# One order for all units, earlier split units, padding from a row: a scheduler change to a fused FFT and SwiGLU kernel

## The chip, the cores and the metric

The kernel runs on one core of one Trainium2 chip. The metric is the device time of one execution in microseconds (us), lower is better. The kernel before takes 624.05 us (median of three runs, 622.47 to 624.16). In what follows PE is TensorE, DVE is VectorE, ACT is ScalarE, POOL is GpSimd and SP is SyncE, which issues most loads and stores.

## The reference, cut to what matters

```python
# x: (8, 3008, 256) float32;  w_gate, w_val: (256, 1536);  w_out: (1536, 256)
X = np.fft.fft(x, axis=1)
X = np.fft.fft(X, axis=2)
x = X.real.astype(np.float32).reshape(8 * 3008, 256)

g = x @ w_gate
silu = g * (1.0 / (1.0 + np.exp(-g)))
val = x @ w_val
return (silu * val @ w_out).astype(np.float32)        # (24064, 256)
```

## The kernel before: the parts that matter here

The Fourier transform over the sequence is done as matmuls with cosine and sine tables, on data folded by symmetry. The transform over the 256 channels is multiplied into the gate and value weights once, at the start (`transform_w`, giving `Wp`, `Wq`, `Wm`). Each batch has a half of its rows (1504) computed directly, and the other half is its mirror image: with P the even and Q the odd part, one half is P·Wp + Q·Wq and its mirror P·Wp − Q·Wq.

The columns are cut into 24 tiles of up to 512, and each tile into 12 units of 128 hidden channels. A unit is computed in one of two ways.

- A **whole** unit takes six matmuls: gate and value, each with Wp, Wq and, for the mirror, Wm (= −2·Wq) accumulated on top. It needs two Silu on ACT and two products on DVE.
- A **split** unit takes five. The mirrored value is worked out on DVE from the value itself: `es` is a copy of the P part with the share of one row of Q added, and the mirrored value is 2·es − v. That needs this row of Q (`br`, then `bc`) broadcast to all partitions by two small loads, and more work on DVE, ACT and POOL. A unit split in its gate as well takes four.

Before the change, tiles 0 to 2 were all whole units, in a fixed order of emission. From tile 3 on, a small list scheduler inside the kernel (`Sched`) ordered them. It keeps one list of operations for each engine, with estimated durations, and picks the operation that can start first within a window.

The first batch's rows arrive in two arrays, `XA` and `XC0`. `XC0` has 60 rows in each half of 64 partitions. The four spare partitions must be zero, because a matmul with a 0/1 matrix ("placing") reads them all. Row 0 of the sequence is loaded into the first spare partition.

```python
    nc.vector.memset(zero, 0.0)
    nc.vector.memset(sel, 0.0)
    q.dma_start(out=XA3[:, 0:4, :], in_=up_block(0, 1, P))
    for a, eng in ((3, nc.scalar), (1, nc.scalar), (2, q), (0, q)):
        eng.dma_start(out=XA3[:, 4 + a, :], in_=down_set(0, a, JA, LA, NA))
    nc.scalar.activation(w0[:, 0, 0:1], zero, AF.Silu)
    xf = XC0.rearrange("p a q d -> p (a q d)")
    nc.scalar.copy(xf, zero.to_broadcast([P, xf.shape[1]]))       # all of XC0 zeroed on ScalarE
    for hi in range(2):
        q.dma_start(out=XC3[64 * hi:64 * hi + NCR, 0:2, :], in_=rows_at(...))
    q.dma_start(out=XC0[NCR:64 + NCR + 1:64, 0:2, 1], in_=rows_at(0, 0, ...))   # row 0
    for hi in range(2):
        for a in range(2):
            q.dma_start(out=XC3[64 * hi:64 * hi + NCR, 2 + a, :], in_=down_set(...))
    ...                                    # XC's padding: four loads from a zero row of XC0

    psA = place(XA, putA, 4, ((psG, "g"), (psV, "v")))
    ...
    half_folded(0, 0)
    psC = place(XC0, putC, 2, ((psO, "o"),))
    half_folded(0, 2)
    ...
    wts0 = [...]       # all eight products for the first third of Wp, Wq
    sums(SC, 1, XC0, psC)
    halves(SBc, SC, 1)
    for fn in wts0:
        fn()
```

The scheduler's rule for when an operation can start:

```python
            def ready(o):
                at = 0.0
                for d in o.deps:
                    x = ops[d]
                    if x.end is None:
                        return None
                    at = max(at, x.end + (0.03 if x.eng == o.eng and x.eng != "SP" else x.lat))
                ...                                             # buffers
                return at
```

The last tile's output matmuls accumulate 12 products for each block of 128 rows, two blocks to a PSUM bank, in the pool `psO` of two banks:

```python
        def product(self, st, pair, j, minus, c, n, f, t):
            if "ps" not in st:
                st["ps"] = psO.tile([P, 2, D], F32, name="o")
            nc.tensor.matmul(st["ps"][:n, j, :], hts[t][minus][:, f, c:c + n], Wo[:, f, :],
                             start=(f == 0), stop=(f == nF - 1))
```

## Time and profile before

| | before |
|---|---|
| median of three runs | 624.05 us |
| span of the profiled run | 621.6 us |
| PE busy | 604.1 us (97%) |
| DVE, ACT, POOL busy | 91%, 85%, 73% |
| first placing of XC0, first gate matmul | 13.33, 23.47 us |
| last matmul starts, span ends | 616.37, 621.57 us |

These are lines of the page of the kernel before: span, busy time of each engine, PE's busy share and granted clock in 40 equal slices (9 is 90% or more), and the chain of work that ended last, by engine and by line.

```profile
span 621.6 us, 12538 instructions
...
PE 604.1 (97%) x4020; PEld 394.0 (63%) x4080; DVE 568.3 (91%) x1042; ACT 526.8 (85%) x999; POOL 453.6 (73%) x421
...
PE   7889999999999999999999999999999999999996
...
PEclk9999999999999999999999999999999999999999
...
PE 88%; DMA 4%; DVE 3%; ACT 2%; issue 2%; POOL 0%; ACTq 0%; SPq 0%; DVEq 0%
PE o L1082 38%; PE g L876 25%; PE v L876 20%; DMA XA<-in_moe_w_val_dram 2%; PE g L1241 2%; PE o L1241 2%; DMA XA<-in_x_dram 1%; DMA XC<-in_x_dram 1%; DVE sv L1028 1%; DVE hp L1038 1%; DVE es L969 0%; PE o L567 0%; PE g L567 0%; ACT sv L1014
```

PE bounds the kernel. Only the first three slices and the last are under 90%, the clock is full throughout, and 88% of the chain is matmuls. So time can be won by fewer matmuls, and at the two ends.

Next are the first 50 us of the kernel before in the waits of PE: who waited for what, us in total, times, longest.

```profile
PE v L876 <- DVE hp L892: 2.3, 5, 0.9
PE g L408 <- DVE rr L331: 1.9, 1, 1.9
...
PE g L876 <- DVE Qt L603: 0.7, 1, 0.7
```

And the first 32 us of its chain (start us, us, what) show what sets the start:

```profile
1.42 7.91 DMA XA<-in_x_dram
...
9.34 0.84 SPq L252
...
10.22 6.21 DMA XC<-in_x_dram
...
16.55 0.71 DVE SC L417 x2
```

Loads do. One of XA's ends at 9.3, and the last of XC0's (L252) is issued then and lands at 16.4. The timeline of the same stretch (start us, us, engine, line, operation) shows the copy that the change takes out, the loads behind it, and the first placing of XC0 and the first gate matmul:

```profile
3.46 1.88 ACT L244 COPY XC<-zero 128x2048 f32<-128x2048 f32 x1
...
5.37 0.82 SPq L246 DMA_DIRECT2D XC<-in_x_dram  x2
...
7.00 4.05 SPq L252 DMA_DIRECT2D XC<-in_x_dram  x4
...
13.33 1.88 PE L408 MATMUL o<-XC,putC 128*128 128x512 f32 x4
...
23.47 0.37 PE L876 MATMUL g<-Pt,Wp 128*128 128x480 bf16 x1
```

Tiles 1 and 2 run from about 50 to 110 us. A row of the windows view gives start and end, length, busy time of PE, of PE's weight loads, of DVE, ACT and POOL with counts, then granted clock, DMA share and GB/s. Kernel before:

```profile
50.00:110.00 60.00, 59.68 (x408) 38.37 (x413) 42.12 (x73) 37.06 (x68) 38.71 (x48) 1.00 0.44 121
```

DVE is busy 42.1 of 60 us there, and PE loses almost nothing.

At the end, the only wait of PE in the kernel before is for an eviction:

```profile
PE o L1082 <- ACT ev L1088: 0.7, 1, 0.7
```

### The profile page before, as it was taken

How to read it: one execution, taken by the hardware profiler on the slowest of the kernel's cores; microseconds unless marked ns; L12 is line 12 of the kernel's file. 1: busy time of each engine (PE TensorE's matmuls, PEld its weight loads, DVE VectorE, ACT ScalarE, POOL GpSimd, SP SyncE). 2: the span in 40 equal slices, each digit the busy share in tenths (PEclk: the TensorE clock that was granted, in tenths of full speed). 3: DMA queues.
4: the chain of work that ended last, by engine and by line, in shares of the span. 5: the costliest groups of instructions: out<-in, count | busy, mean ns of one | idle time of the engine just before them, and what ended most of it. 6: DMA issues, size and time to landing. Idle time of an engine off the chain costs nothing.

```text
span 621.6 us, 12538 instructions
## 1 busy us (share of the span) xinstructions
PE 604.1 (97%) x4020; PEld 394.0 (63%) x4080; DVE 568.3 (91%) x1042; ACT 526.8 (85%) x999; POOL 453.6 (73%) x421
## 2 busy tenths in 40 slices
PE   7889999999999999999999999999999999999996
PEld 5346666666666666566666666666666666666684
DVE  7798567999999999999999999999999999999981
ACT  7686666899889889888898889998898988989992
POOL 8896955888877989886988779868786434545551
PEclk9999999999999999999999999999999999999999
DMA  9973346345326223546153113144211211111121
GB/s 228 127 136 96 114 114 172 107 140 140 96 62 153 61 64 100 146 97 145 52 136 97 58 45 95 46 109 112 61 60 36 61 44 54 51 53 53 41 69 61
DMA packets 50237, 57.39 MB, mean 92 GB/s; under 512 B 7170, under 2 KB 37226, under 8 KB 50154
## 3 DMA queue, kind: packets, MB, share of 16 engines
q1 hardware_dynamic: 46698, 53.70, 31.9%
q0 software_dynamic: 3184, 2.36, 3.1%
q8 instruction: 32, 0.52, 0.4%
q10 hardware_dynamic: 288, 0.52, 0.3%
q14 instruction: 35, 0.29, 0.2%
HBM read 29.39 MB, written 24.65 MB: 87 GB/s over the span
## 4 chain that ended last, share of the span: by engine, by line
PE 88%; DMA 4%; DVE 3%; ACT 2%; issue 2%; POOL 0%; ACTq 0%; SPq 0%; DVEq 0%
PE o L1082 38%; PE g L876 25%; PE v L876 20%; DMA XA<-in_moe_w_val_dram 2%; PE g L1241 2%; PE o L1241 2%; DMA XA<-in_x_dram 1%; DMA XC<-in_x_dram 1%; DVE sv L1028 1%; DVE hp L1038 1%; DVE es L969 0%; PE o L567 0%; PE g L567 0%; ACT sv L1014 0%; ACT ev L1088 0%
## 5 line engine op out<-in xcount | busy, mean ns | idle before, releaser
L1035 POOL TENSOR_TENSOR hm<-sv 128x1024 bf16<-128x1024 f32 (+2 forms) x126 | 234.1, 1858 | 130.3 <-ACT sv L1014 61.2
L1028 DVE SCALAR_TENSOR_TENSOR sv<-es,v 128x512 f32<-128x512 f32 (+2 forms) x252 | 168.3, 668 | 3.4 <-PE v L876 1.6
L1082 PE MATMUL o<-Wo,hm 128*128 128x256 bf16 (+2 forms) x1140 | 169.3, 273 | 1.4 <-ACT ev L1088 0.7
L1082 PE MATMUL o<-Wo,hp 128*128 128x256 bf16 (+1 forms) x1140 | 169.6, 273 | 0.6
L1038 DVE TENSOR_TENSOR hp<-sp,v 128x512 bf16<-128x512 f32 (+2 forms) x249 | 166.2, 668 | 2.9 <-ACT sp L1011 2.4
L1082 PEld LDWEIGHTS <-hm 128*128 128x128 bf16 (+2 forms) x1140 | 111.6, 98 | 63.2 <-issue 2.4
L1082 PEld LDWEIGHTS <-hp 128*128 128x128 bf16 (+1 forms) x1140 | 112.0, 98 | 60.0 <-issue 0.9
L944 ACT ACTIVATE sp<-g 128x512 f32<-128x512 f32 (+2 forms) x189 | 112.8, 597 | 27.4 <-PE g L876 22.5
L1014 ACT ACTIVATE sv<-g 128x512 f32<-128x512 f32 (+2 forms) x189 | 124.3, 659 | 5.2 <-PE g L876 4.2
L876 PE MATMUL g<-Pt,Wp 128*128 128x512 bf16 (+2 forms) x282 | 105.6, 375 | 0.2
L876 PE MATMUL v<-Pt,Wp 128*128 128x512 bf16 (+2 forms) x279 | 104.5, 375 | 0.5
L969 DVE SCALAR_TENSOR_TENSOR es<-bc,w,v 128x512 f32<-128x512 bf16 (+2 forms) x126 | 91.8, 728 | 2.4 <-PE o L1082 1.3
L876 PE MATMUL g<-Qt,Wq 128*128 128x512 bf16 (+2 forms) x248 | 92.4, 374 | 1.3 <-DVE Qt L603 0.7
L920 ACT ACTIVATE v<-bc,w 128x512 f32<-128x512 bf16 (+2 forms) x126 | 87.7, 696 | 1.1 <-DVE hp L1038 0.5
L876 PE MATMUL g<-Qt,Wm 128*128 128x512 bf16 (+2 forms) x222 | 83.1, 374 | 0.6
L967 ACT COPY es<-v 128x512 f32<-128x512 f32 (+2 forms) x126 | 74.3, 589 | 2.7 <-PE v L876 2.4
L876 PEld LDWEIGHTS <-Wp 128*128 128x128 bf16 x576 | 56.2, 98 | 27.0 <-issue 5.3
L1088 ACT COPY ev<-o 128x512 f32<-128x512 f32 x90 | 54.4, 605 | 10.8 <-PE o L1082 5.9
L876 PE MATMUL v<-Qt,Wm 128*128 128x512 bf16 (+2 forms) x162 | 60.7, 375 | 2.3 <-DVE hp L892 2.3
L876 PE MATMUL v<-Qt,Wq 128*128 128x512 bf16 (+2 forms) x162 | 60.7, 375 | 0.7 <-DVE es L969 0.6
L876 PEld LDWEIGHTS <-Wq 128*128 128x128 bf16 x450 | 44.0, 98 | 26.8 <-issue 0.9
L876 PEld LDWEIGHTS <-Wm 128*128 128x128 bf16 x387 | 37.9, 98 | 17.8
(182 smaller groups left out, 719.0 us busy)
## 6 DMA issues: line engine op xcount, KB each, us to landing
out_dram<-ev SPq DMA_DIRECT2D x96, 128.0 KB
XA<-in_x_dram SPq DMA_DIRECT2D x30, 256.0 KB
XA<-in_x_dram SPq DMA_DIRECT2D x112, 64.0 KB
XC<-in_x_dram SPq DMA_DIRECT2D x32, 120.0 KB
XC<-in_x_dram SPq DMA_DIRECT2D x105, 32.0 KB
bc<-br SPq DMA_DIRECT2D x19, 128.0 KB
St<-Fc SPq DMA_DIRECT2D x14, 128.5 KB
out_dram<-ev SPq DMA_DIRECT2D x12, 120.0 KB
```

Of the source, the lines that this page charges most:

```text
L876: nc.tensor.matmul(ps[:, :n], Wt[:, gv, fs], src[:, :n], start=start, stop=stop, skip_group_check=True)
L920: nc.scalar.activation(T_[kv][:, :w], bc[t][:, :w], AF.Copy, scale=w0[:, 1, f:f + 1])
L944: nc.scalar.activation(T_[ksp][:, :w], T_[kg][:, :w], AF.Silu)
L967: nc.scalar.copy(T_[kes][:, :w], T_[kv][:, :w])
L969: nc.vector.scalar_tensor_tensor(T_[kes][:, :w], bc[t][:, :w], w0[:, 1, f:f + 1], T_[kv][:, :w], op0=Alu.mult, op1=Alu.add)
L1014: nc.scalar.activation(sv()[:, f % 2, w - 1::-1, 1], T_[kgm if by_dve else kg][:, :w], AF.Silu)
L1028: nc.vector.scalar_tensor_tensor(sv()[:, f % 2, w - 1::-1, 0], T_[kes][:, :w], 2.0, T_[kv][:, :w], op0=Alu.mult, op1=Alu.subtract)
L1035: nc.gpsimd.tensor_tensor(hts_(t)[1][:, f - 1:f + 1, :w], sv()[:, :, :w, 1], sv()[:, :, :w, 0], op=Alu.mult)
L1038: nc.vector.tensor_tensor(hts_(t)[0][:, f, :wp], T_[ksp][:, :wp], T_[kv][:, :wp], op=Alu.mult)
L1082: nc.tensor.matmul(st["ps"][:n, j, :], hts[t][minus][:, f, c:c + n], Wo[:, f, :], start=(f == 0), stop=(f == nF - 1))
L1088: nc.scalar.copy(ev[:, 0:len(pair), :], st["ps"][:, 0:len(pair), :])
L1241: nc.tensor.matmul(st[q][:, cols], l, r_, start=(i == 0), stop=(i == len(mms) - 1), skip_group_check=True)
```

## The change

The intent is to let the scheduler order everything from the first unit, to save matmuls in tiles 1 and 2 by splitting 14 units of theirs, to free the start of a 1.88 us copy and to shorten the end. In detail:

1. `Sched` orders all units of tiles 0 to 2, and also the later weight products and the tables; `run` takes starting offsets for each engine.
2. Fourteen units of tiles 1 and 2 become split (one of them in the gate too).
3. The padding of XC0 and XC comes by loads of 256-byte pieces from a zero row of `sel`. XC0's loads use two queues, and row 0 goes last.
4. Half of the products for the first third of the weights move behind the second half of the transform.
5. The last tile's outputs use the PSUM banks of all three pools.
6. Windows, shifts and the choice of seeded units are re-tuned.
7. In `ready`, a matmul that depends on an earlier matmul of PE is no longer booked 0.03 us late.

```diff
     nc.vector.memset(sel, 0.0)
+    nc.scalar.activation(w0[:, 0, 0:1], zero, AF.Silu)
+    zrow = sel.bitcast(F32)[1:2, :]
+
+    def zeros(X, hi):
+        dst = X.rearrange("p a q d -> p (a q d)")[64 * hi + NCR:64 * hi + 64, :]
+        return dict(out=dst.rearrange("p (k n) -> p k n", n=P // 2),
+                    in_=zrow.unsqueeze(1).to_broadcast([1, (64 - NCR) * dst.shape[1] * 2 // P, P // 2]))
+
     q.dma_start(out=XA3[:, 0:4, :], in_=up_block(0, 1, P))
-    for a, eng in ((3, nc.scalar), (1, nc.scalar), (2, q), (0, q)):
+    for a, eng in ((3, nc.scalar), (2, q), (1, nc.scalar), (0, q)):
         eng.dma_start(out=XA3[:, 4 + a, :], in_=down_set(0, a, JA, LA, NA))
-    nc.scalar.activation(w0[:, 0, 0:1], zero, AF.Silu)
-    xf = XC0.rearrange("p a q d -> p (a q d)")
-    nc.scalar.copy(xf, zero.to_broadcast([P, xf.shape[1]]))
     for hi in range(2):
-        q.dma_start(out=XC3[64 * hi:64 * hi + NCR, 0:2, :], ...)
+        q.dma_start(**zeros(XC0, hi))
+    ...
+    for hi, what in ((0, 2), (1, 2), (0, 0), (1, 0), (0, 1), (1, 1)):
+        (q, nc.scalar)[hi if what != 1 else 0].dma_start(**xc0(hi, what))
     q.dma_start(out=XC0[NCR:64 + NCR + 1:64, 0:2, 1],
                 in_=rows_at(0, 0, [[2 * R * D, 2], [R * D, 2], [1, D]]))
     ...
+    pts(putC, putC, scalar1=pcol, scalar2=1.0, op0=Alu.is_equal, op1=Alu.mult)     # POOL
-    vts(putC, putC, scalar1=pcol, scalar2=None, op0=Alu.is_equal)                  # DVE
     ...
-    for fn in wts0:
-        fn()
+    for k, (pool, nm) in enumerate(((psV, "v"), (psG, "g"))):
+        half_w(0, k, pool, nm)
     ...
     transform(0, 0, (1,), acc)          # the order here is unfolded, transform, then:
+    half_w(1, 0, psO, "o")
+    half_w(1, 1, psO, "o")
     ...
-    W_PE = 2.5
-    W_ACT = 4.0
+    W_PE = 2.0
+    W_ACT = 2
-    SH_EG = 0.0          (SH_HP, SH_HM, SH_PUT = 0.0)
+    SH_EG = 0.5          (SH_HP = 0.5, SH_HM = -0.5, SH_PUT = -1)
     ...
-                    at = max(at, x.end + (0.03 if x.eng == o.eng and x.eng != "SP" else x.lat))
+                    at = max(at, x.end + (x.lat if x.eng != o.eng or x.eng == "SP" else 0.0 if x.eng == "PE" else 0.03))
     ...
+    SPLIT_EARLY = ((1, 2), (1, 3), (1, 4), (1, 5), (2, 0), (2, 1), (2, 4), (2, 5), (2, 6), (2, 7), (2, 8), (2, 9), (2, 10), (2, 11))
+    GATE_EARLY = ((1, 5),)
-    SEED, SEED_END = (4, 5, 6, 8, 9, 11), (2, 3, 5, 7, 9, 11)
-    POOL, POOL_END = (), (8,)
+    SEED, SEED_END = (4, 5, 6, 8, 9, 11), (1, 3, 5, 7, 9, 11)
+    POOL, POOL_END = (), (6, 8)
     ...                                  # whole_a, whole_b, weight_op, angle_op, ...: as scheduled operations
-        direct = i < FIRST               # and all that was emitted directly
+        row_at = {0: 11, 2: 99}.get(t, 6)     # in which unit the broadcast row of the next tile is issued
     ...
-    owork = OWork(prev[0])
+    owork = OWork(prev[0], ((psG, "g"), (psV, "v"), (psO, "o")))
     owork.run(len(owork.steps))
-    S.run()
+    S.run({'DVE': 1.2, 'ACT': 0.7, 'POOL': 14.0, 'PE': 0.0})
```

## The prediction

> **What bounds the kernel now.** TensorE does, once it is fed. The page has PE busy 97% of a 621.6 us span at full clock, and the chain of waits is 88% PE. The Trainium skill (Perfetto Trace Analysis, Identifying the Most-Contended Engine) calls matmul busy share a bad measure because matmuls are pipelined; so I use start-to-start spacing in the timeline: 216 ns for 512 columns, 203 for 480, 109 for 256, back to back. The program's 4074 matmuls at that spacing (four-fold for the six float32 ones) need about 597 us. The other 25 us:
> - 0 to 50 us: about 11 us without a matmul. PE waits for x to land (1.9), for a weight copy on DVE (1.2), for the first Qt (0.9), and in tile 0 for DVE products that free the v banks (1.1, 0.7 and smaller) and for late weights (0.5). DVE is 87 to 93% busy from 30 to 50 us.
> - 50 to 606 us: some 6 us in all; about half is the small one-row matmuls.
> - The end: 0.67 us waiting for an eviction to free an o bank, six gaps of 0.1 us between alternating groups, then 5 us for two evictions and their stores.
>
> **What the change does.**
> 1. Fourteen units of tiles 1 and 2 become split: each drops one 512-column value matmul, and one drops a gate matmul too. 15 x 0.216 = 3.2 us less PE. They add es on DVE (0.73 each), move work to ACT and POOL, but there (50 to 110 us) DVE is only 60 to 70% busy and ACT 60%, and PE 99.5%: nearly all 3.2 us is on the path.
> 2. The whole-value units, weight products and tables get ordered by the scheduler. In tile 0 DVE work is unchanged and nearly saturated, so only part of the roughly 5 us lost between 24 and 50 us comes back: my estimate is 1.5 us.
> 3. Start: the 1.88 us zero copy on ACT that held the first XC load until 5.37 us goes; those loads start by about 3 us on two queues. But the DMA view is already near full share from 2 to 16 us, and the first-half weights landed at 19.05, as late as the XC part. Half the fc=0 products move behind the second accumulation and fill the wait for Qt. The padding becomes 256-byte pieces; the skill (DMA: Bandwidth & Descriptors, Specifications) puts line rate at 512 bytes or more, a small drag. Estimate: 1 us gained.
> 4. End: no wait for an o bank, ungrouped alternation gone, one smaller eviction last: 1.5 us gained.
> 5. Re-tuned windows and shifts over tiles 3 on: PE is already back to back; plus or minus 1 us, estimate 0.5 gained.
>
> Sum 3.2 + 1.5 + 1 + 1.5 + 0.5 = 7.7 us: **616.5 us**, 8 in 10 between 612.5 and 620. Faster by over 2%: 0.08; within 2%: 0.91; slower: 0.01.
>
> **What would show it right or wrong.** PE record count about 7 lower and busy time about 3 to 5 us lower; the first gate matmul (23.5 us before) at about 22.5; the first output matmul of tile 0 about 2.5 us earlier; no eviction wait before the last 36 matmuls, and last matmul to span end under 5 us; PE 99% in windows after 50 us.
>
> **What would make it wrong.** The broadcast row for tile 1 landing late behind loads, so that PE, in order, stalls at the first split unit; DVE or POOL falling behind in tiles 1 and 2; the 256-byte padding delaying XC; or a startup freed much more than I think, which would bring over 2%.

## The result, and the profile after

The time did not move: 624.59 us (median of four runs, 624.44 to 625.28) against 624.11 (four runs of the kernel before in the same rounds, 622.47 to 625.17). The ratio is 1.0012, with a 95% interval of 0.9989 to 1.0035. Here and below a ratio is the mean time of one kernel's fast runs over that of the other's fast runs of the same rounds, so it is not quite the ratio of the medians quoted beside it.

The same lines of the page, now of the kernel after:

```profile
span 622.8 us, 12518 instructions
...
PE 601.7 (97%) x4012; PEld 393.9 (63%) x4073; DVE 576.9 (93%) x1054; ACT 527.6 (85%) x1001; POOL 472.2 (76%) x432
...
PE   6799989999999999999999999999999999999997
...
PEclk9799999999999999999999999999999999999999
...
PE 84%; DVE 6%; DMA 4%; issue 2%; SPq 2%; ACT 2%; POOL 1%; DVEq 0%; ACTq 0%; POOLq 0%
PE o L1144 35%; PE g L904 22%; PE v L904 19%; DVE es L1027 2%; PE g L1287 2%; PE o L1287 2%; DMA XC<-in_x_dram 2%; DMA XC<-sel 1%; DVE sv L1088 1%; SPq L142 1%; DMA XA<-in_x_dram 1%; PE v L1144 1%; PE o L413 1%; SPq L140 1%; PE g L581 1%
```

PE has less to do, as intended (604.1 to 601.7 us), and yet the span is no shorter. Two things are new: the clock is not full in the second slice, and the chain holds loads from `sel`, which are the padding, and `es`. To see where the time went, I mark when the n-th `hp` product (the product, on DVE or POOL, that ends the direct half of a unit) ends. There are 288 of them, one for each unit. These times and the counts of matmuls by stretch are worked out from the instruction records of one profiled execution of each kernel.

| us | before | after | difference, after less before |
|---|---|---|---|
| start to 1st product | 28.11 | 34.17 | +6.1 |
| 1st to 12th (tile 0) | 20.83 | 21.09 | +0.3 |
| 12th to 48th (tiles 1, 2 and 3) | 81.93 | 81.12 | −0.8 |
| 48th to 288th | 477.34 | 475.62 | −1.7 |
| 288th to the end | 13.36 | 10.82 | −2.5 |
| span | 621.57 | 622.82 | +1.3 |

The start loses 6.1 us, and all the rest together wins 4.8. (The line of the 48th to 288th product is taken up again in the fifth group of experiments: most of its gain is not the change's.) These are the first 32 us of the chain after, to hold against the chain before:

```profile
0.74 5.46 DMA XA<-in_x_dram
...
6.22 8.06 DMA XC<-sel
...
14.29 4.90 DMA XC<-in_x_dram
19.19 0.24 issue
19.43 3.75 PE o L413 x4
```

Now the start is a row of loads, one after the other. The padding of XC0's second half is issued at 6.2, when a load of XA has ended, and lands at 14.3. Only then can the load of row 0 go out, because it writes into the padded partition; it lands 4.9 us later, although it carries 4 KB. The placing follows at 19.43 (13.33 before) and takes 3.75 us in place of 1.88, because the clock is halved from 14.0 to 24.2 us. The waits of PE (first 50 us) and of SP's own queue (first 60 us) of the kernel after say the same:

```profile
PE o L413 <- DMA XC<-in_x_dram: 4.7, 1, 4.7
PE v L468 <- ACT EOb L481: 2.5, 1, 2.5
PE g L413 <- DVE rr L336: 1.6, 1, 1.6
```

```profile
SPq L251 <- DMA XA<-in_x_dram: 2.7, 1, 2.7
...
SPq L261 <- DMA XC<-sel: 2.1, 2, 1.1
```

L251 is the padding and L261 the load of row 0. The padding uses no data of XA: in the records it waits for the semaphore (101) that this load of XA counts up, and takes the same one itself. In the kernel before, the last four loads of XC0 (L252) likewise wait for the semaphores of loads of XA that they then take. The wait sits on the issuing queue, as the Trainium skill says (DMA: Bandwidth & Descriptors, Anatomy of one DMA): DMA engines don't wait for semaphores, the sequencer that issues does. The half clock agrees with the skill in part (TensorE: Matmul & The Clock Gate, What's actually happening), which has the clock fall to 1.2 GHz after an idle window of about 3.4 us and come back after a busy one. The stretch at half clock lasts 10.2 us, three times 3.4. But it begins at 14.0 us, after the wait of 2.5 us alone; in the 3.4 us before it PE was still busy for 1.0 us. The wait of 4.7 us falls inside it.

The first gate matmul comes at 30.68 in place of 23.47, as this line of the timeline after shows:

```profile
30.68 0.37 PE L904 MATMUL g<-Pt,Wp 128*128 128x480 bf16 x1
```

Tiles 1 and 2 (50 to 110 us) in the windows view after, and PE's waits in that stretch:

```profile
50.00:110.00 60.00, 57.43 (x368) 36.22 (x372) 51.74 (x93) 36.77 (x69) 49.80 (x55) 1.00 0.49 124
```

```profile
PE v L904 <- DVE es L1027: 2.0, 2, 1.7
```

DVE went from 42.1 to 51.7 us of 60, and PE from 59.7 to 57.4. A look at tile `bc`, the broadcast row that `es` needs, shows why that wait arose: the load went out at 83.0 us, behind row loads of the next batch on the same queue, and the first `es` of tile 2 waited for it:

```profile
L1423 SPq DMA_DIRECT2D bc<-br x1: 607/607/607, 83.0 to 83.0; - x1
...
  DMA bc<-br: 3.5, 1
...
  PE v L904: 1.7, 1
```

At the end no wait of PE is listed any more.

### The profile page after: what moved, and what is told of

Same layout as the page of the kernel before. It is cut to its first block, busy times and chain, and to the rows that moved or that the text cites. A ratio compares the mean times of both kernels' runs of the same rounds, so it can differ in the third digit from the quotient of the medians.

```text
span 622.8 us, 12518 instructions
## 1 busy us (share of the span) xinstructions
PE 601.7 (97%) x4012; PEld 393.9 (63%) x4073; DVE 576.9 (93%) x1054; ACT 527.6 (85%) x1001; POOL 472.2 (76%) x432
## 4 chain that ended last, share of the span: by engine, by line
PE 84%; DVE 6%; DMA 4%; issue 2%; SPq 2%; ACT 2%; POOL 1%; DVEq 0%; ACTq 0%; POOLq 0%
PE o L1144 35%; PE g L904 22%; PE v L904 19%; DVE es L1027 2%; PE g L1287 2%; PE o L1287 2%; DMA XC<-in_x_dram 2%; DMA XC<-sel 1%; DVE sv L1088 1%; SPq L142 1%; DMA XA<-in_x_dram 1%; PE v L1144 1%; PE o L413 1%; SPq L140 1%; PE g L581 1%
## 5 line engine op out<-in xcount | busy, mean ns | idle before, releaser
L1095 POOL TENSOR_TENSOR hm<-sv 128x1024 bf16<-128x1024 f32 (+2 forms) x133 | 247.7, 1862 | 119.3 <-ACT sv L1074 65.4
L1088 DVE SCALAR_TENSOR_TENSOR sv<-es,v 128x512 f32<-128x512 f32 (+2 forms) x266 | 177.8, 669 | 1.7 <-issue 0.6
L1098 DVE TENSOR_TENSOR hp<-sp,v 128x512 bf16<-128x512 f32 (+2 forms) x260 | 174.1, 670 | 3.2 <-ACT sp L1071 2.4
L1144 PE MATMUL o<-Wo,hm 128*128 128x256 bf16 (+1 forms) x1128 | 166.4, 273 | 0.7
L1144 PE MATMUL o<-Wo,hp 128*128 128x256 bf16 (+1 forms) x1104 | 165.6, 273 | 0.4
L1144 PEld LDWEIGHTS <-hp 128*128 128x128 bf16 (+2 forms) x1140 | 112.1, 98 | 62.4 <-issue 3.9
L1002 ACT ACTIVATE sp<-g 128x512 f32<-128x512 f32 (+2 forms) x202 | 120.0, 595 | 32.9 <-PE g L904 21.6
L1074 ACT ACTIVATE sv<-g 128x512 f32<-128x512 f32 (+2 forms) x202 | 131.5, 652 | 7.8 <-PE g L904 5.1
L1027 DVE SCALAR_TENSOR_TENSOR es<-bc,w,v 128x512 f32<-128x512 bf16 (+2 forms) x140 | 101.9, 730 | 5.1 <-DMA bc<-br 3.5
L904 PE MATMUL v<-Qt,Wm 128*128 128x512 bf16 (+2 forms) x148 | 55.4, 374 | 0.5 <-DVE hp L942 0.5
```

Of the source, the lines that this page charges most:

```text
L904: nc.tensor.matmul(ps[:, :n], Wt[:, gv, fs], src[:, :n], start=start, stop=stop, skip_group_check=True)
L1002: nc.scalar.activation(T_[ksp][:, :w], T_[kg][:, :w], AF.Silu)
L1027: nc.vector.scalar_tensor_tensor(T_[kes][:, :w], bc[t][:, :w], w0[:, 1, f:f + 1], T_[kv][:, :w], op0=Alu.mult, op1=Alu.add)
L1074: nc.scalar.activation(sv()[:, f % 2, w - 1::-1, 1], T_[kgm if by_dve else kg][:, :w], AF.Silu)
L1088: nc.vector.scalar_tensor_tensor(sv()[:, f % 2, w - 1::-1, 0], T_[kes][:, :w], 2.0, T_[kv][:, :w], op0=Alu.mult, op1=Alu.subtract)
L1095: nc.gpsimd.tensor_tensor(hts_(t)[1][:, f - 1:f + 1, :w], sv()[:, :, :w, 1], sv()[:, :, :w, 0], op=Alu.mult)
```

## The experiments

Each kernel below has six runs, in five timed rounds and one profiled run, against the kernel before on the same chip. The medians of before lay between 623.73 and 624.77. The expectations call the theories by letters that they had at the time; what the theories say is told ahead of each group. "Placing" is the first placing of XC0, "gate" the first gate matmul.

### First: is it the padding?

Theory P: the padding from a row of `sel` holds the load of row 0 and with it PE. Its rivals are the cold clock, and the order of the program.

**e1_copy_xc0.** After, with XC0's padding by the copy on ScalarE again.

```diff
-    for hi in range(2):
-        q.dma_start(**zeros(XC0, hi))
+    xf = XC0.rearrange("p a q d -> p (a q d)")
+    nc.scalar.copy(xf, zero.to_broadcast([P, xf.shape[1]]))
```

> The changed kernel, but the four spare partitions of each half of XC0 are zeroed again by the copy on ScalarE instead of by 256-byte pieces copied from one row. Theory P (padding): the pieces land at 14.3 us, the short load of row 0 waits for them and lands at 19.2, and the placing matmuls wait for that; without them the placing starts by about 14 us, the first gate matmul comes at 23 to 25 us (31.1 in the changed kernel) and the time is 617 to 619 us. Rival L (loads): the two-queue order of the XC0 loads, or the weight copy moved to POOL, makes the start late; then the first gate matmul stays near 31 us and the time stays above 623 us.

622.51 us (619.37 to 624.54), ratio 0.9975 [0.9954, 0.9997]. Placing came at 14.73 and gate at 25.32, down from 19.43 and 30.68. The start was nearly as theory P says, but the time fell by less, and the runs spread over 5 us. (For the changed kernel the expectation has 31.1 where the first gate matmul starts at 30.68; 31.11 is the start of a later one.)

**e2_before_selpad.** Before, with only the padding of the change.

```diff
-    xf = XC0.rearrange("p a q d -> p (a q d)")
-    nc.scalar.copy(xf, zero.to_broadcast([P, xf.shape[1]]))
+    for hi in range(2):
+        q.dma_start(**zeros(XC0, hi))        # as in the change; XC's padding likewise
```

> The kernel before, with only the padding of XC0 and XC taken from the one row, as the changed kernel has it. Theory P: the start slips by 4 to 8 us here too, 628 to 632 us against 624.1. Rival L: 624 to 625 us, since its loads are on one queue as before.

628.32 us (625.95 to 629.22), ratio 1.0057 [1.0040, 1.0075]; placing 18.39, gate 28.96. The padding alone, put into the old kernel, costs 3.6 us (0.57% of 624.5). The chain of this kernel over the first 32 us holds the pieces from 3.50 to 14.12:

```profile
3.50 10.62 DMA XC<-sel
...
18.39 3.49 PE o L411 x4
```

Behind them the last four loads of XC0 were issued between 14.8 and 17.6 us, which was 7.0 to 10.2 in the kernel before. The clock was at half from 18.7 to 22.1 us.

**e3_copy_both.** As e1, with the padding of XC as before too.

```diff
-        q.dma_start(**zeros(XC, hi))
+        for k in range(2):
+            q.dma_start(out=X3c[64 * hi + NCR:64 * hi + 64, 8 * D * k:8 * D * (k + 1)], in_=...)   # zero row of XC0
```

> As the first run of this call, and the padding of XC as before too (8192-byte pieces out of XC0). If only the padding of XC0 matters: within 1 us of that first run. If the 512 small pieces of the XC padding hold up the later weights as well: 1 to 3 us faster than it.

623.13 us (620.81 to 627.41), 0.9982 [0.9955, 1.0008]. That is e1 within the noise, so XC's padding matters little.

**e4_warm.** After, with 120 more filler matmuls before and during the wait, so that the clock stays full.

```diff
-    warm(20)
+    warm(60)
...
+    warm(80)
     psC = place(XC0, putC, 2, ((psO, "o"),))
```

> The changed kernel, with 120 more filler matmuls while PE waits for XC0 (40 after the first placing, 80 before the second). The trace of the changed kernel grants half the clock from 14 to 24 us. Theory C: the half clock costs about 2 us on the path (the second placing took 3.75 us against 1.88 before, the next accumulations are slower too); with the filler the clock stays at 1.0 and the time falls to 622 to 623 us. Rival: the vector work after each placing sets the pace, so the clock is off the path: within 0.5 us of the changed kernel's 624.6.

624.07 us (622.17 to 626.52), 0.9991 [0.9969, 1.0012]. The clock was full throughout, placing stayed at 19.62, and gate came at 28.5, 2.2 us earlier than after. So the half clock made some 2 us of the late start, and the wait made the rest. The time did not follow; in this trace PE then waited 3.3 us for `es`.

### Second: what remains once the padding is mended?

Theory B: the late broadcast row (`br`, `bc`) of tile 2 costs what e1 failed to win. The rivals are the clock, and the move of `putC` to POOL.

**f1_bc** (after, with the row of tile 2 issued earlier), **f2_copy_bc** (that with e1), **f3_copy_bc_warm** (f2 with 40 more filler matmuls), **f4_putc** (f3 with `putC` back on DVE):

```diff
-        row_at = {0: 11, 2: 99}.get(t, 6)
+        row_at = {0: 11, 1: 2, 2: 99}.get(t, 6)          # f1, f2, f3, f4
-    warm(20)
+    warm(60)                                             # f3, f4
-    pts(putC, putC, scalar1=pcol, scalar2=1.0, op0=Alu.is_equal, op1=Alu.mult)
+    vts(putC, putC, scalar1=pcol, scalar2=None, op0=Alu.is_equal)      # f4
```

> The changed kernel, with the two small loads that spread tile 2's first row (br, bc) issued earlier, right after those of tile 1, instead of behind the XC loads of the next fold. Theory B: the stall of PE at 86 us (1.9 us in the trace, es waiting for bc, up to 3.5 us in other runs) is the queue's doing; it goes, and the time falls by 2 to 3 us to 621.5 to 623, and the runs of one call differ less. Rival: the vector engine is behind there anyway; the wait moves to another releaser and the time stays at 624.5.

> XC0 zeroed by the copy on ScalarE (the first run of the first call) and the early row of tile 2 together. If the two delays are separate they add: 618 to 620 us, and its runs lie within 2 us of each other where those of the copy alone lay between 619.4 and 624.5. If something else made that spread: a spread of 4 us or more again.

> As f2, with 40 more filler matmuls after the first placing, so that PE does not idle for 2.5 us before the first folded products. Theory C (clock): the half clock from 15 to 19 us goes, the first gate matmul comes 1.5 us earlier (25.3 in the copy run, so 23.8) and the time is 616.5 to 618. Rival: no change against f2.

> As f3, with the comparison that makes putC back on DVE where the kernel before has it. If its move to POOL delays the first folds by its 0.75 us and that is on the path: 0.5 us faster than f3, first gate matmul at 23.2. If not: the same within 0.3 us.

| | median us (range) | ratio [95%] | gate |
|---|---|---|---|
| f1_bc | 624.68 (621.42 to 626.38) | 1.0013 [0.9991, 1.0035] | 28.34 |
| f2_copy_bc | 620.36 (617.64 to 624.16) | 0.9960 [0.9937, 0.9983] | 23.93 |
| f3_copy_bc_warm | 620.40 (618.10 to 621.93) | 0.9944 [0.9924, 0.9964] | 25.35 |
| f4_putc | 618.78 (617.46 to 624.27) | 0.9940 [0.9908, 0.9972] | 24.02 |

The early row took the longest wait for `es` in the trace from 1.7 to 0.9 us, but f1 alone won no time, so what the late row costs in time is not shown. Over all traces it does what it is for: in the seven with the late row of tile 2 (after, e1, e3, e4, h1, h2, k1) the longest wait of PE for `es` was 1.5 to 6.8 us, in the ten with the early row at most 0.9. With the padding mended and the row early, f2 is 0.52% faster than after, and the intervals don't overlap. The steps from f2 to f4 are within each other's intervals. I call f4 the mended kernel. It beats both kernels: it is 0.6% under before, 5.0 us by the medians.

### Third: can the pieces be made cheap, and what are splits and the end worth?

Theory Q: the pieces are only at the wrong place in the queue, and issued first they are harmless. Theory S: they are slow in themselves wherever they go.

**h1_first.** After, with XC0's padding issued ahead of the loads of XA.

```diff
+    for hi in range(2):
+        q.dma_start(**zeros(XC0, hi))
     q.dma_start(out=XA3[:, 0:4, :], in_=up_block(0, 1, P))
...
-    for hi in range(2):
-        q.dma_start(**zeros(XC0, hi))
```

> The changed kernel, with the two padding copies of XC0 issued first of all, before the loads of XA, and nothing else moved. Theory Q (queue): the pieces are late because they stand in the queue behind 2 MB of XA, and the short row-0 load then waits for them and goes through the queue a second time; issued first they land early, the row-0 load waits for nothing of theirs, and the placing of XC0 starts at 14.5 to 16.5 us (19.4 in the changed kernel); time 621 to 623. Rival S (size): 256 small pieces[...] are slow by themselves; then XA is late instead, the placing starts after 18 us, and the time stays at 624 to 625.

628.71 us (623.12 to 631.63), 1.0078 [1.0043, 1.0113]. Now the loads of XA came late. PE's waits over the first 40 us of this kernel:

```profile
PE g L412 <- DMA XA<-in_x_dram: 8.0, 1, 8.0
```

The first placing of XA moved from 6.3 to 13.5 us, that of XC0 came at 20.66. Theory Q fails. What S says of XA came true: here the pieces delayed the loads behind them. The time rose by more than S had forecast.

**h2_big.** After, with padding in pieces of 8192 bytes in place of 256.

```diff
-        q.dma_start(**zeros(XC0, hi))
+        q.dma_start(out=X0[64 * hi + NCR:64 * hi + 64, :], in_=zbig.unsqueeze(1).to_broadcast([1, 64 - NCR, 8 * D]))
```

> The changed kernel, with the padding of XC0 and XC taken from one 8192-byte row (zeroed on ScalarE in 2 us) instead of 256-byte pieces; same number of copies for XC0 at the same place in the queue. Theory Q: still behind XA, the row-0 load still waits: the placing starts at 18 us or later, 623.5 to 625.5. Rival S: the pieces were the cost: placing at 15.5 or earlier, 621 to 622.5.

626.93 us (623.41 to 628.92), 1.0045 [1.0015, 1.0076]; placing 17.67, gate 29.22. Bigger pieces brought the placing forward by 1.8 us and no time. That is between the forecasts of Q and S, so the small size is at most a part of the cost. Why the padding takes so long to land (in after its second half, 32 KB, from 6.2 to 14.3 us) stays open; that each half goes to four partitions only is a rival that no run tests. This trace had the longest single wait for `es` but one, 5.8 us.

**g1_nosplit.** The mended kernel with the 14 units whole.

```diff
-    SPLIT_EARLY = ((1, 2), (1, 3), ...)
-    GATE_EARLY = ((1, 5),)
+    SPLIT_EARLY = ()
+    GATE_EARLY = ()
```

> The mended kernel (copy on ScalarE, early row, filler, putC on DVE; 618.8) with the 14 units whole again: 15 more matmuls of 512 columns, 3.2 us of PE. If the split units are all gain, as I predicted: 622. If DVE, which is 90 to 99% busy from 50 to 120 us with them, gives some back (PE waits for es and hp 2 us in all): 619.5 to 621.

620.16 us (618.54 to 622.98), 0.9948 [0.9921, 0.9974]. That is 0.0008 from f4, 0.5 us, within the noise. From the first to the 288th product g1 took 578.02 us and f4 577.50. The split units save 3.2 us of matmuls; 0.5 us is what the times and the traces show for it, and the times do not tell that from nothing.

**g2_tail.** The mended kernel with the old PSUM pool for the last outputs.

```diff
-    owork = OWork(prev[0], ((psG, "g"), (psV, "v"), (psO, "o")))
+    owork = OWork(prev[0])
```

> The mended kernel with the last outputs in the o banks alone, as before. Last matmul to the end of the span and the wait before it: 1.5 to 3 us slower, 620.3 to 621.8; PE waits 0.6 us for an eviction before the last 36 matmuls again.

621.22 us (618.67 to 625.13), 0.9963 [0.9929, 0.9997]. By the times alone the pools looked worth 1.4 us (the difference of the ratios). The trace contradicts that: from the 288th product to the last matmul it took 6.78 us, against 6.77 in f4, and from there to the end 3.68 in both. PE had no wait at the end either. Its loss lies before the 48th product, where PE waited once for 2.0 us for ACT. So with the rest of the change in place the pools do nothing here, and something else shortened the end.

### Fourth: the load of row 0, the windows, the choice of units

Theory W: the load of row 0, waiting for the padding of its partition, is the second half of the late placing.

**k1_norowwait.** After, with row 0 loaded ahead of the padding and three partitions padded in place of four (so a quarter less padding too). It is wrong (relative error 0.04), since what lies around row 0 in its partition is then not zero.

```diff
-        q.dma_start(**zeros(XC0, hi))
+    q.dma_start(out=X0[NCR:64 + NCR + 1:64, :], in_=rows_at(0, 0, ...))
+    ...    # zeros for partitions NCR + 1 to NCR + 3 of each half
...
-    q.dma_start(out=XC0[NCR:64 + NCR + 1:64, 0:2, 1], in_=rows_at(0, 0, ...))
```

> The changed kernel with a wrong result on purpose: the partition of row 0 is filled whole by its load (with other rows of x in the place of zeros), ahead of the padding, and the padding covers the three other partitions of each half. So the row-0 load no longer waits for padding and no load stands behind the pieces but those of XC0. Theory W (second pass): the row-0 load's wait for the pieces and its own 4.9 us through the queue are most of the delay; the placing of XC0 starts at 15 to 16.5 us (19.4 in the changed kernel), time 621.5 to 623.5. Rival S (the pieces and what they push back): placing after 17.5 us, 624 to 625.

622.18 us (619.89 to 628.56), 0.9992 [0.9954, 1.0031]. Placing came at 16.09 in place of 19.43, which is what W forecast: waiting behind the padding is up to 3.3 of the 6.1 us (a quarter less padding is in it too). The times are too wide to say more; the profiled run was the slowest of them, with one wait of 6.8 us for `es`.

**j1_row** (the mended kernel with row 0 loaded first of XC0's loads), **j2_windows** (the mended kernel with the old windows and shifts) and **j3_spread** (the mended kernel with 12 split units in spaced pairs):

```diff
+    (load of row 0)                                              # j1: ahead of the loop below
     for hi, what in ((0, 2), (1, 2), (0, 0), (1, 0), (0, 1), (1, 1)):
...
-    W_PE = 2.0
-    W_ACT = 2
+    W_PE = 2.5                                                   # j2
+    W_ACT = 4.0                                                  # j2, and SH_EG, SH_HP, SH_HM, SH_PUT = 0.0
...
-    SPLIT_EARLY = ((1, 2), (1, 3), (1, 4), (1, 5), (2, 0), (2, 1), (2, 4), ..., (2, 11))
+    SPLIT_EARLY = tuple((t, f) for t in (1, 2) for f in (2, 3, 6, 7, 10, 11))        # j3, the list written shorter
+    GATE_EARLY = ()                                              # j3
```

> The mended kernel (copy on ScalarE, early row of tile 2, filler, putC on DVE) with the row-0 load first among the loads of XC0 instead of last. In its trace the placing of XC0 starts at 15.1 us, 1.4 us after PE was ready; in three sister runs between 15.0 and 16.6. If the short last load is what it waits for: placing at 13.8 to 14.5, time about 1 us less, 617 to 618.5. If the other XC0 loads are as late: no change.

> The mended kernel with the scheduler's windows and shifts as before (PE 2.5, ACT 4.0, all shifts zero). My prediction gave the new ones 0.5 us; its trace gained about 1.8 us between the 48th and the 288th unit over the kernel before. If they make that gain: 620 to 621. If it came from elsewhere: 618.5 to 619.5.

> The mended kernel with 12 split units set apart (f 2, 3, 6, 7, 10, 11 of tiles 1 and 2) instead of 14 in two dense stretches, no gate split. PE has 3 matmuls more (0.65 us). If the dense stretches overload DVE, its waits (about 2.5 us in 50 to 110 us) shrink to 1 us or less and the time is 617.5 to 618.5; if any split costs DVE as much as it saves PE: 619.5 to 620.5, no better than whole units (620.2).

| | median us (range) | ratio [95%] | 1st to 288th product |
|---|---|---|---|
| j1_row | 619.74 (617.44 to 622.18) | 0.9932 [0.9908, 0.9956] | 577.68 |
| j2_windows | 620.64 (617.91 to 624.34) | 0.9955 [0.9923, 0.9987] | 577.60 |
| j3_spread | 618.50 (617.05 to 621.79) | 0.9925 [0.9901, 0.9948] | 576.33 |

j1 brought the placing to 13.77 us, and no more time than f4. Its first gate matmul came at 26.26, later than the 24.02 of f4, after a wait of 1.4 us for DVE and with the clock at half from 21.0 to 24.4 us; so an earlier placing alone is not an earlier start. j2 shows that the windows are worth nothing in the steady stretch: 475.57 us from the 48th to the 288th product, against 475.61 with the new ones. j3 is the fastest kernel by the ratio. With the splits spaced out, the trace wins 1.2 us over f4. The windows rows of f4, then of j3, for 50 to 110 us:

```profile
50.00:110.00 60.00, 57.66 (x377) 36.47 (x376) 51.87 (x89) 36.18 (x69) 50.89 (x53) 1.00 0.55 148
```

```profile
50.00:110.00 60.00, 59.28 (x385) 38.07 (x391) 51.93 (x88) 39.02 (x72) 51.31 (x53) 1.00 0.57 148
```

DVE has the same load in both, but PE loses 2.3 us in f4 and 0.7 in j3. (g1, without splits, has PE at 59.95 and DVE at 43.31.) So the mean load of DVE does not tell what PE loses. How close together the extra work falls is the likely reason; j3 also has two split units fewer and no gate split, which no run sets apart.

### Fifth: what shortened the end?

Theory G: the line in `ready`, which no longer books a matmul 0.03 us late behind another of PE. With the 0.03, the builder finds some other block's matmul that can start a little earlier, and so alternates between blocks that should be finished one after the other. Theory T: the PSUM pools, or the moved seeded units.

**m1_pe_gap** (the mended kernel with the old line) and **m3_before_nogap** (the kernel before with the new line alone):

```diff
-                    at = max(at, x.end + (0.03 if x.eng == o.eng and x.eng != "SP" else x.lat))
+                    at = max(at, x.end + (x.lat if x.eng != o.eng or x.eng == "SP" else 0.0 if x.eng == "PE" else 0.03))
```

(This is m3; m1 is its reverse on the mended kernel.)

> The mended kernel (putC on VectorE, copied padding, early row, filler), with one line of the order's builder put back: a matmul that follows another on TensorE is again booked 0.03 us late, as before the change. Theory G (this rule, not the PSUM pools, made the end shorter): the built order then alternates two blocks of output matmuls at the end; the trace shows about 8 us from the last hp product to the last matmul (6.8 without) and about 4.5 to 5.2 us from there to the end (3.7 without), so 2 to 3 us more, median near 621, ratio 0.996 to 0.999. Theory T (the PSUM pools or the moved seeded units did it): the end stays at 6.8 and 3.7 us, median 618 to 619.5, ratio 0.991 to 0.995. Both: start as in the mended kernel, first gate matmul 24 to 26 us.

> The kernel before with that one line of the change alone: a matmul that follows another on TensorE is booked without the 0.03 us. Theory G: the end gets as short as after the change, 6.8 us and 3.7 to 4 us in place of 8.2 and 5.2, with no other part of the change; median 621 to 622, ratio 0.994 to 0.998. If it also makes the steady stretch shorter, the trace shows 0.5 to 1.5 us less between the 48th and the 288th hp product (477.3 before). Theory T: the end as before, no change of time (ratio 0.998 to 1.002). Start as before in both: first gate matmul 23 to 25 us.

m1: 625.59 us (621.59 to 626.77), 1.0000 [0.9973, 1.0026]. m3: 620.26 us (619.01 to 622.31), 0.9938 [0.9920, 0.9955].

| us | before | m3 | mended (f4) | m1 |
|---|---|---|---|---|
| start to 1st product | 28.11 | 27.43 | 27.72 | 30.32 |
| 1st to 48th | 102.76 | 103.14 | 101.89 | 101.69 |
| 48th to 288th | 477.34 | 475.99 | 475.61 | 475.66 |
| 288th to last matmul | 8.16 | 6.78 | 6.77 | 7.33 |
| last matmul to end | 5.20 | 3.80 | 3.68 | 4.81 |

One line put into the kernel before gives nearly all that the mended kernel gives: 0.62% or 3.9 us, of which its trace shows 2.8 at the end. The trace is also 1.35 shorter in the steady stretch, as the expectation had thought possible, but that cannot be put down to the line. e2 has the old line, and differs from the kernel before in its opening alone; it took 476.10 us there. The profiled execution of before fell 1.2 us behind e2 between its 96th and 132nd product (in it PE waited once for `es`, 0.6 us at 251.9 us), and kept that distance.

Theory G stands. Theory T falls as the main cause, since the line alone gives the short end (10.6 us from the 288th product, 13.4 before, 10.5 in f4). But m1, with the rest of the change and the old line, took 12.1, so without the line some other part of the change is worth 1.2 us there. The timelines of m1 and of m3, last output matmuls, show how the line does this. First m1, alternating:

```profile
610.95 0.60 PE L1144 MATMUL o<-Wo,hm 128*128 128x256 bf16 x4
611.48 0.62 PE L1144 MATMUL g<-Wo,hm 128*64 128x256 bf16 x4
612.03 0.61 PE L1144 MATMUL o<-Wo,hm 128*128 128x256 bf16 x4
612.58 0.62 PE L1144 MATMUL g<-Wo,hm 128*64 128x256 bf16 x4
```

Then m3, with all 36 in one row:

```profile
609.40 4.21 PE L1082 MATMUL o<-Wo,hm 128*128 128x256 bf16 x36
```

In m3 the full bank is finished first and evicted at 612.26, while PE still does the last block; only the 64-row eviction at 613.69 comes after the last matmul. In the kernel before both evictions came after it, at 617.00 and 617.48.

In the mended kernel the old line costs 1.7 us at the end and nothing in the steady stretch (m1). Its time rose by more than that, 0.6%. In its profiled run 2.6 us of that came at the start, where m1 and f4 have the same program; the traces of the other runs are not kept.

## Why the prediction was wrong

The prediction was 616.5 us, 7.6 below before; the measured change is +0.1%, outside the range. It came as five terms.

**The start (its item 3, 1 us gained): this step failed.** "The padding becomes 256-byte pieces; [...] a small drag" and "the 1.88 us zero copy on ACT that held the first XC load until 5.37 us goes" were both wrong. The copy seems to have cost little: in the kernel before, the last four loads of XC0 wait for loads of XA in any case, the last until 9.3 us (argued from the trace; no run takes out the copy by itself). The first gate matmul moved from 23.5 to 30.7 us, and the padding makes about 5.4 of these 7.2 (30.7 to 25.3 in e1; 23.5 to 29.0 in e2). It costs 3.6 us of time when put into the old kernel (e2), and f2, with the copy back and an early row, wins 0.52%, 3.3 us, over after. The mechanism is a chain: the pieces wait for a load of XA (2.7 us), take until 14.3 us to land, hold back the load of row 0 (up to 3.3 us of the placing, k1), and leave PE idle, so that it goes on at half clock (2.2 us of the first gate matmul, e4; these parts overlap). Neither the order (h1) nor the size of the pieces (h2) mends it. What did the damage was less the bytes than the place in a chain of dependent loads. I had listed "the 256-byte padding delaying XC" as a risk and sized it by the rate for small pieces alone. In the traces this step makes 7.1 us (6.1 lost in place of 1 gained) of the 9.0 between the forecast (7.7 gained) and the span (1.3 lost).

The padding is not the whole of the late start. The seven profiled runs with row padding in any form had the first gate matmul at 28.0 to 30.7 us, the eleven of the changed kernel with the copy at 23.9 to 27.0 (25.6 on average), and the two of the old program with the copy at 22.4 and 23.5. So some 2 to 3 us of the late start belong to the rest of the new opening; no run parts them further.

**The split units (item 1, 3.2 us): mis-sized.** The matmuls are gone, but only 0.5 us of time came of it, within the noise (g1 against f4); where the units are spaced out it was 1.7 in the traces (j3 against g1, first to 288th product). I argued from DVE at 60 to 70% over 60 us. The added work falls on a few stretches where DVE is the limit, and PE then waits for it: 2.3 us lost in f4. In the trace of after, PE waited another 1.7 us for the late broadcast row. I had foreseen that for tile 1, and it came in tile 2.

**Ordering of tile 0 (item 2, 1.5 us): in part there, and hidden by the marks.** From the first to the 12th product it took 0.3 us longer. But PE did 29 matmuls more in that stretch (24 of them the small one-row ones, which came after it before), and its idle time fell from 1.9 to 1.0 us. From the first gate matmul to the first output matmul of tile 0 it took 23.1 us, 26.2 before.

**The steady stretch (item 5, 0.5 us): not shown.** The traces gained 1.7 us, but not by the windows (j2), and not by the line in `ready`, since m1 keeps the gain without it. 1.2 us of it is also in e2 (476.10), which has the old line and the old order there; that much is what the one profiled execution of before lost. How often it loses that is not known, as only one of its executions is kept. The other 0.5 us stays open.

**The end (item 4, 1.5 us): the size was too small and one of the causes wrong.** The trace gained 2.5 us. "Ungrouped alternation gone" was right; "no wait for an o bank" was true too, but the pools that were to bring it add nothing once the line is there (g2), and the line alone gives 2.8 us (m3).

Of the checks, these came true: the last matmul to the end is under 5 us (4.05), no eviction wait is left there, and the program has 7 matmul records fewer. For that the weight loads are the better witness (4080 to 4073): PE's own records (4020 to 4012) are not complete, and e2 and m3, with the matmuls of before, show 4080 and 4017. So its busy time (2.4 us less, forecast 3 to 5), which also holds matmuls at half clock, says little. These did not: the first gate matmul, the first outputs of tile 0 (53.8 us, 49.7 before; but 47.4 in f4, with the start mended), and PE at 99% after 50 us (57.4 of 60 from 50 to 110).

So two things nearly cancel: one line in the scheduler gives 3.9 us alone (2.8 of them seen at the end of its trace, the rest not located), the padding takes 3.6 us alone, and all the rest is worth about 1 us either way, which the timing here does not resolve. The mended kernel (618.78), the spaced one (618.50) and the kernel before with the one line (620.26) are not told apart by their intervals.

What stays open, besides the above: single runs of the variants of the changed kernel spread over 4 to 9 us where those of before spread over 2 to 5 (the four of the changed kernel itself over 0.8). Kernels with the same opening (f4, g1, g2, j2, j3, m1) had their first product between 27.7 and 30.3 us, so part of it is in the start. Where the longer runs lost the rest is not known, as only the first run of each keeps its trace. The clocks narrow it down. In most of the changed kernels the longer runs have the lower mean clock (in f4 four runs at 1.000 took 617.5 to 619.4 us, those at 0.994 and 0.997 took 622.4 and 624.3); the runs of before show no such tie. In the traces of e3, h2 and k1 half clock came with the wait for `es` of 3.5 to 6.8 us. So long waits of PE in the longer runs are likely, but not shown.

## What to carry to other kernels

When a load is replaced or added at the start, follow the chain of what waits for it, and for whose completion it waits, and size it from there; its bytes and rate say little. Extra work on an engine with 30% of its time free still stalled the busiest engine here, most likely because it came in a lump, so look at short windows and try to spread it. Before a gain between two traces is given a cause, hold it against a third trace with the same code in that stretch: here that took back 1.2 us. And read every line of a scheduler's diff: the smallest one, of 0.03 us, was worth more than the 14 split units, and only putting it into the old kernel by itself showed it.

## What the Trainium skill lacked or had wrong

- DMA: Bandwidth & Descriptors (Anatomy of one DMA) gives a fixed cost of about 2 us for a transfer, measured on the GpSimd path. Here a 4 KB load on SP's queue took 4.9 us from issue to landing, with other loads in flight. Its four packets of 1024 bytes ran from 17.7 to 17.9 us, 3.4 us after its issue at 14.3. The page (Latency and other measured facts) has an HBM access of 2 us at high load, and no figure for a short load behind others in its queue, which was what mattered.
- The same page (Specifications) puts full rate at pieces of 512 bytes or more. That led me to call 256-byte pieces a small drag. Pieces of 8192 bytes brought the placing only from 19.4 to 17.7 us and won no time (h2). The page gives no figure for how long such copies hold back other loads: issued first, they moved the first placing of XA from 6.3 to 13.5 us (h1). It does treat how many DMA engines a copy of a given shape gets, which the prediction did not use; no run tests that for these pieces.
- TensorE: Matmul & The Clock Gate (What's actually happening) has the clock fall after an idle window of about 3.4 us. Here it fell with PE not idle for that long: in the 3.4 us before, PE was busy for 1.0 us in after, 1.4 in e1 and 1.8 in j1. A wait of 2.5 us was followed by half clock in after and in e1, one of 2.6 us in f2 was not. The page calls the ramp under 1% of a typical span. That holds here, but 0.35% of the span was 2.2 us of the first gate matmul (e4), as much as other terms of this change.
- Perfetto Trace Analysis (Optimization Strategy) says that the most-contended engine can change between regimes of a kernel, and that mixing them can help. It does not say how short such a regime can be: within the same 60 us, with DVE busy for 86% in both cases, PE lost 2.3 us with the extra work in lumps (f4) and 0.7 with it spaced out and two units fewer (j3).
